# A routed expert layer on one Trainium2 core: weight splits of short and double units, a third branch place, and a copy outside its branch

## The chip, the cores and the metric

One of the eight cores of a Trainium2 chip runs the whole program, once per launch. The metric is the device time of that execution in microseconds (us). Engines: TensorE (PE), VectorE (DVE), ScalarE (ACT), GpSimd (POOL), and SyncE (SP), which issues most transfers.

## The reference

Three layers in a row. An attention between 2048 tokens and 128 states gives 2176 rows of 512; a dense layer follows; then a layer with eight experts, of which each row uses the one with the highest score:

```python
def _moe2_ref(x, expert_emb, tau, w1, w2):
    ...
    expert_idx = np.argmax(logits, axis=1)
    ...
    for e in range(E):
        mask = expert_idx == e
        ...
        h = np.maximum(x[mask] @ w1[e], 0.0)
        out[mask] = gate_w[mask, None] * (h @ w2[e])
```

Here x is 2176 x 512, w1[e] 512 x 1024 and w2[e] 1024 x 512, all float32. For the inputs timed here the experts get 568, 519, 0, 544, 512, 32, 0 and 1 rows.

## The kernel before

A float32 product is made from rounded parts: every operand is split into a high part (ACT copies it to `fp32r`, line 80) and a low part (DVE subtracts, line 81), and three matmuls high x high, low x high, high x low are added up in PSUM (`mm3`, lines 112 to 114).

The routed layer works in **units** U of up to 256 rows of one expert. Unit 0 and 1 are planned early. From unit 2 on the units' experts and shapes are numbers that the chip works out itself, and every engine branches on them (`tc.If`). A unit is **double** (129 or more rows, kind 2), single (65 to 128, kind 1) or **half** (up to 64, kind 0). With the row counts above the units are, in order, with the expert in brackets: 2 double (0), 3 half (3), 4 half (0), 5 double (4), 6 double (1), 7 double (4), 8 half (1), 9 half (5), 10 double (3), 11 half (7), 12 double (3). Unit 12 (`END`) is the last.

Each unit does, in the order of the program: PE turns the next unit's gathered rows (`xt_turns`, `gt<-ident,xg`); the first product h = x W1 (`chosen(U, 0)`); then `middle`: the next unit's x is split into `xth`, `xtl` by ACT and DVE (`xt_split`), GpSimd gathers rows for a later unit, and `fill(U, 0)` splits weights for later units; then the second product y (`chosen(U, 1)`), scaling by the gate (`scale`, tile `ys`) and scattering; then `fill(U, 1)`, the last piece of the weight split. In a double unit (`double_up`) the first product is made in four groups of 24 matmuls in three PSUM banks, each followed by `grouped`: ReLU on ACT (`hth`, line 1147) and the low part on DVE (`htl`, line 75). In a single or half unit (`single_up`) x is the stationary operand, h comes in two halves of 512 columns, ACT copies each out (`hs`, line 1221), PE turns it (`turn`, line 1229 for halves), and ACT and DVE make `hth` from that. A half unit keeps high and low parts of its 64 rows side by side in the 128 lanes, so that the two halves of y must be added at the end: ACT copies the upper 64 lanes (line 1254), DVE adds them (line 1255).

The weights are held in two places, of which unit U uses number U % 2. A unit with a new expert needs W1 (`w1h`, `w1l`, four pieces of 128 x 1024) and W2 (`w2h`, `w2l`, four pieces) split before; the unit ahead does that, steered by a code `due_[U]`: 3 splits W1 and W2 for unit U+1, 2 splits W2 alone (W1 was made one unit earlier), 1 splits W1 for unit U+2, 0 nothing. `fill(U, 0)` makes W1 and three pieces of W2, `fill(U, 1)` the fourth. The codes, and the experts that SP is to fetch next (`fetch`), are computed by DVE in `codes` and lie in the table `plan_`. Instructions of an engine run in the program's order; nothing reorders them here.

Of the kernel before, what the change touches and what calls it, by code (L numbers as in the profile page):

```python
# [11 lines left out]
I32 = mybir.dt.int32  # L12
# [44 lines left out]
def body(tc, x, state, w_in, w_out, ee, tau, w1, w2, out):  # L57
# [58 lines left out]
    with stack:  # L116
# [583 lines left out]
        ctl = rt.tile([P, 2, NU], I32, name="ctl")  # L700
        plan_ = dots.rearrange("p t e -> p (t e)")[:, P // 2 : P // 2 + 3 * NU].bitcast(I32).rearrange("p (r u) -> p r u", r=3)
        ef = rt.tile([P, NU], F32, name="ef")
# [113 lines left out]
        def plan():  # L816
# [87 lines left out]
            def codes():  # L904
# [117 lines left out]

        def fetch(U):

            for part in (1, 2):
                cell = plan_[0:1, part, U : U + 1]
                code = nc.values_load(cell, engines=[ET.SP], min_val=0, max_val=NE)
                with tc.If(code < NE):
                    fetch_part(nc.values_load(cell, engines=[ET.SP], min_val=0, max_val=NE - 1), part)

        PIECES = range(3), range(3, 4)

        def fill(U, half):

            with tc.If(due_[U] > 1):
                if not half:
                    with tc.If(due_[U] > 2):
                        split_all(U + 1, 1)
                split_all(U + 1, 2, PIECES[half])
            if U + 2 <= END:  # L1040
                with tc.If(due_[U] == 1):  # L1041
                    split_all(U + 2, 1, PIECES[half])
# [11 lines left out]

        kind, kp, kf, due_, hT, HP = {}, {}, {}, {}, [], P // 2
        fold = dots.rearrange("p t e -> p (t e)")[:, 0:HP]

        def kinds(U):

            kind[U] = nc.values_load(ctl[0:1, 1, U : U + 1], engines=UENG, min_val=0, max_val=2, skip_runtime_bounds_check_because=BOUND)  # L1060
            kp[U], kf[U] = (bass.RuntimeValue.of_register_unchecked(bass.RegisterHandles([kind[U].val[e] for e in engines]), min_val=0, max_val=2) for engines in ([ET.PE], FENG))

        def dues(U):
            if U < END:
                due_[U] = nc.values_load(plan_[0:1, 0, U : U + 1], engines=FENG, min_val=0, max_val=3, skip_runtime_bounds_check_because=BOUND)

# [63 lines left out]
        def ends(U):  # L1130
            if U == END:
                ix_[U] = [dots[:, NT - 1, r : r + 1].bitcast(I32) for r in range(2)]
# [69 lines left out]
        def double_out(U):  # L1202
            for r in range(1 if U == END else 2):
                down(U, [r])
                scale(U, r)
                scatter(U, r)

        def second(U):
            q = U % 2
            return [(hth[U][k // 4][:, k % 4 * P : (k % 4 + 1) * P], htl[U][k // 4][:, k % 4 * P : (k % 4 + 1) * P], W2H[q, k // 2][:, k % 2, :], W2L[q, k // 2][:, k % 2, :]) for k in range(NFE)]  # L1210

        def single_up(U):
            q, y, ts = U % 2, y_[U][0], second(U)
            h, tr = hs_[U], (hq[U][2], hq[U][0])

# [3 lines left out]

            def leave(m):  # L1220
                A.activation(h[m], hq[U][m], AF.Copy)

            def turn(m):
                with tc.If(kp[U] > 0) as w:
                    for k in range(4):
                        T.transpose(tr[m][:, k * P : (k + 1) * P], h[m][:, k * P : (k + 1) * P], ident)
                with w.Else():
                    for k in range(4):
                        T.matmul(tr[m][:, k * P : k * P + HP], h[m][:, k * P : (k + 1) * P], fold, start=True, stop=True)
                with tc.If(kf[U] > 0) as w:  # L1230
                    positive(hth[U][m], htl[U][m], tr[m])
                with w.Else():
                    positive(lanes(hth[U][m], 0), lanes(hth[U][m], 1), lanes(tr[m], 0))

            high(hq[U][0], terms(0), True)
            low(U, hq[U][0], terms(0))
            leave(0)
            high(hq[U][1], terms(1), True, range(5))
            turn(0)
            high(hq[U][1], terms(1), False, range(5, 8))  # L1240
            low(U, hq[U][1], terms(1))
            leave(1)
            high(y, ts[0:4], True, range(4))
            turn(1)
            high(y, ts[0:4], False, range(4, 8))
# [202 lines left out]
        with tc.manual_schedule():  # L1448
# [68 lines left out]
            kinds(2)  # L1517
            middle(1)
            store(1)
            fill(1, 1)  # L1520
            fetch(1)
            nblk = nc.values_load(ctl[0:1, 1, 0:1], min_val=UMIN, max_val=NU)
            for U in range(2, U1):
# [5 lines left out]
                with cond(U):  # L1529
# [22 lines left out]
            for g in LATE:  # L1552
                late.enter_context(tc.If(nblk > g[0]))
                for U in g:
# [12 lines left out]
                    ends(U)  # L1567
                    chosen(U, 1)
            late.close()
            for r in range(2):  # L1570
# [29 lines left out]
```

## Time and profile before

| | us |
|---|---|
| median of 3 runs | 698.29 (697.58 to 699.22) |
| profiled execution | 694.48 |
| its span, first to last instruction | 692.6 |
| PE busy in the span | 664.3 (96%) |
| DVE, ACT, POOL busy | 480.8, 437.8, 196.6 |

The rows further down come from the profiled execution. In a timeline a row gives the start, the duration, engine, line, operation, what it writes and reads, its count, and in brackets how long the engine was idle before it and what ended that. Matmuls overlap: the time that PE takes for one is the step from its start to that of the next.

### The profile page before, as it was taken

What the parts mean: (1) busy time and instruction counts of PE and PEld (TensorE: products, weight loads), DVE (VectorE), ACT (ScalarE), POOL (GpSimd) and SP (SyncE); (2) the same over time, 40 slices, a digit from 0 to 9 for tenths busy, and PEclk for the clock granted to TensorE, in tenths of its full rate; (3) what the DMA queues carried; (4) which work ended last, traced back from release to release, by engine and by line L of the source; (5) the groups of instructions that cost most, each with busy time, mean ns of one, the idle gap of its engine ahead of it and who ended that gap; (6) DMA issues with size and microseconds to landing.
All of it is one profiled execution on the core that took longest, in us unless ns stands there. A gap on an engine that the chain in (4) does not pass through costs nothing. (4 is left out here: it accounts for less than half of the span.)

```text
span 692.6 us, 11937 instructions
## 1 busy us (share of the span) xinstructions
PE 664.3 (96%) x3833; PEld 565.5 (82%) x3833; DVE 480.8 (69%) x1044; ACT 437.8 (63%) x771; POOL 196.6 (28%) x165
## 2 busy tenths in 40 slices
PE   8898999999999999999999999999989999988995
PEld 8798887777888888888887878998868889767794
DVE  5987798989567786586669888995655722357731
ACT  5877998999788767766786777520544512245520
POOL 2777265553000130030014041233243220332101
PEclk9989999999999999999999999999999999999998
DMA  7663053432010254441122356445695370554401
GB/s 191 158 160 118 32 149 121 126 122 62 1 61 1 59 140 108 92 85 38 62 77 61 131 167 187 126 108 183 207 361 188 120 254 31 186 155 145 166 3 35
DMA packets 58239, 82.71 MB, mean 119 GB/s; under 512 B 25050, under 2 KB 35802, under 8 KB 58148
## 3 DMA queue, kind: packets, MB, share of 16 engines
q1 hardware_dynamic: 54388, 70.31, 34.3%
q0 software_dynamic: 3760, 11.30, 5.0%
q8 instruction: 43, 0.70, 0.4%
q14 instruction: 48, 0.39, 0.2%
HBM read 65.32 MB, written 13.65 MB: 114 GB/s over the span
## 5 line engine op out<-in xcount | busy, mean ns | idle before, releaser
L112 PE MATMUL acc<-woh,gh 128*128 128x512 f32 x272 | 108.5, 403 | 2.0 <-ACT gh L80 1.6
L113 PE MATMUL acc<-wol,gh 128*128 128x512 f32 x272 | 107.5, 396 | 0.0
L114 PE MATMUL acc<-woh,gl 128*128 128x512 f32 x272 | 93.9, 398 | 0.9 <-DVE gl L81 0.9
L112 PE MATMUL hp<-xth,w1h 128*128 128x256 f32 x256 | 72.6, 284 | 1.2 <-DVE htl L75 1.2
L114 PE MATMUL hp<-xth,w1l 128*128 128x256 f32 x256 | 72.1, 281 | 1.5 <-DVE w1l L81 1.5
L113 PE MATMUL hp<-xtl,w1h 128*128 128x256 f32 x256 | 71.9, 281 | 0.6 <-DVE xtl L81 0.6
L1147 ACT ACTIVATE hth<-hp 128x512 fp32r<-128x512 f32 (+1 forms) x34 | 17.8, 533 | 72.7 <-PE hp L114 53.1
L112 PEld LDWEIGHTS acc<-woh,gh 128*128 128x128 f32 x272 | 51.2, 188 | 14.9 <-ACT gh L80 5.0
L523 ACT ACTIVATE er<-h,mb__104 128x512 f32<-128x512 f32 x68 | 46.5, 684 | 25.5 <-PE h L114 22.0
L114 PEld LDWEIGHTS acc<-woh,gl 128*128 128x128 f32 x272 | 50.6, 188 | 14.6 <-DVE gl L81 3.9
L113 PEld LDWEIGHTS acc<-wol,gh 128*128 128x128 f32 x272 | 51.2, 188 | 10.1
L529 DVE TENSOR_TENSOR er<-er 128x512 f32<-128x512 f32 x56 | 40.3, 720 | 21.6 <-ACT er L523 20.9
L1053 POOL DMA_INDIRECT xg<-x1d,perm x26 | 36.4, 1399 | 65.6 <-DVEq L1041 12.8
L552 ACT ACTIVATE h<-er,mb__104 128x512 f32<-128x512 f32 x68 | 47.3, 695 | 8.4 <-DVE er L529 4.8
L112 PE MATMUL h<-xh,mh 128*128 128x512 f32 x128 | 51.3, 401 | 0.4 <-ACT xh L80 0.4
L113 PE MATMUL h<-xl,mh 128*128 128x512 f32 x128 | 50.7, 396 | 0.4 <-DVE xl L81 0.4
L114 PE MATMUL h<-xh,ml 128*128 128x512 f32 x128 | 50.5, 394 | 0.0
L553 ACT ACTIVATE er<-er,mb__104 128x512 f32<-128x512 f32 x68 | 49.3, 725 | 1.4
L114 PEld LDWEIGHTS hp<-xth,w1l 128*128 128x128 f32 x256 | 48.2, 188 | 2.1 <-DVE w1l L81 2.1
L1162 POOL DMA_INDIRECT out<-ys,ix x19 | 22.3, 1176 | 96.8 <-DVE ix L1165 25.7
L112 PEld LDWEIGHTS hp<-xth,w1h 128*128 128x128 f32 x256 | 48.2, 188 | 1.6 <-DVE htl L75 1.4
L113 PEld LDWEIGHTS hp<-xtl,w1h 128*128 128x128 f32 x256 | 48.2, 188 | 0.9 <-DVE xtl L81 0.8
(486 smaller groups left out, 1740.9 us busy)
## 6 DMA issues: line engine op xcount, KB each, us to landing
w<-in_moe_w_in SPq DMA_DIRECT2D x16, 512.0 KB, 4.1
w<-in_moe_w_out SPq DMA_DIRECT2D x16, 512.0 KB, 3.5
es<-in_moe_w SPq DMA_DIRECT2D x32, 256.0 KB, 2.9
sg<-in_moe_w SPq DMA_DIRECT2D x12, 512.0 KB
sd<-in_moe_w SPq DMA_DIRECT2D x12, 512.0 KB
se<-in_moe_w SPq DMA_DIRECT2D x12, 512.0 KB
xn<-in_x SPq DMA_DIRECT2D x32, 128.0 KB, 3.3
md<-mr SPq DMA_DIRECT2D x28, 128.0 KB, 2.4
```

What stands on the lines that cost most here:

```text
L112: T.matmul(o, lh, rh, start=first, stop=False)
L113: T.matmul(o, lh, rl, start=False, stop=False)
L114: T.matmul(o, ll, rh, start=False, stop=last)
L523: A.activation(z, h, AF.Tanh, scale=0.5, bias=mb_[:, 0:1])
L529: V.tensor_tensor(out=z, in0=z, in1=z, op=ALU.mult)
L552: A.activation(r, z, AF.Square, scale=QS, bias=mb_[:, 1:2])
L553: behind["ACT"] = A.activation(z, z, AF.Square, scale=QS, bias=mb_[:, 2:3])
L1053: G.indirect_dma_start(out=xg[U][r], out_offset=None, in_=x1d[: (T1 if U < U0 else NT) * P + 1, :], in_offset=bass.IndirectOffsetOnAxis(ap ...
L1147: A.activation(hi, i, AF.Relu)
L1162: G.indirect_dma_start(out=out[:, :], out_offset=bass.IndirectOffsetOnAxis(ap=ix_[U][r], axis=0), in_=ys_[U][r], in_offset=None, bounds_ch ...
```

## The change

Four things change.

First, `codes` knows two more codes. Where unit U is half or single (`kk` below 2), unit U+1 is double, and the old code is 2 or more, the new code is 7 minus the old one: 4 for 3, 5 for 2. With 4, `fill` splits W1 alone; with 5, nothing. W2 is split inside the double unit instead, after its second group. A fourth row of `plan_` holds the experts whose W2 is then fetched later, inside that double unit.

Second, the unit's branch on its shape stands in three places: `chosen(U, 1)` is the second product alone, `chosen(U, 2)` scaling and scattering. In a half unit the turning of the second half of h moves from the first place to the second, so that on ACT and DVE it stands behind `xt_split` and ahead of `fill(U, 0)`, which moved out of `middle`; the register loads of `kinds` and `dues` come ahead of `fill(U, 0)` too.

Third, ACT's copy of the upper half of y stands ahead of `scale`, outside the branch on half units, which only DVE takes now.

Fourth, the row numbers of unit `END` get tiles of their own, since the fourth row of `plan_` takes their place.

```diff
@@ codes
-                tt(plan_[:, 0, 0 : NU - 2], a[:, 1 : NU - 1], soon[:, 2:NU], ALU.add)
+                tt(b[:, 0 : NU - 2], a[:, 1 : NU - 1], soon[:, 2:NU], ALU.add)
+                V.tensor_copy(plan_[:, 0, 0:U0], b[:, 0:U0])
+                c, put, other = b[:, U0 : NU - 2], room(NL - 2), room(NL - 2)
+                tsc(put, kk[:, 0 : NL - 2], 2.0, ALU.is_lt)
+                stt(put, kk[:, 1 : NL - 1], 2.0, put, ALU.is_ge, ALU.mult)
+                stt(put, c, 2.0, put, ALU.is_ge, ALU.mult)
+                stt(other, put, 7.0, c, ALU.mult, ALU.subtract)
+                tt(plan_[:, 0, U0 : NU - 2], other, c, ALU.max)
...
-                tsc(plan_[:, 2, 1 : NU - 2], a[:, 2 : NU - 1], float(NE), ALU.add)
+                tt(other, a[:, U0 + 1 : NU - 1], put, ALU.mult)
+                tsc(plan_[:, 3, U0 : NU - 2], other, float(NE), ALU.add)
+                tsc(plan_[:, 2, 1:U0], a[:, 2 : U0 + 1], float(NE), ALU.add)
+                stt(plan_[:, 2, U0 : NU - 2], a[:, U0 + 1 : NU - 1], float(NE), other, ALU.add, ALU.subtract)
@@ fill
-                    with tc.If(due_[U] > 2):
+                    with tc.If(due_[U] > 2), tc.If(due_[U] < 5):
                         split_all(U + 1, 1)
-                split_all(U + 1, 2, PIECES[half])
+                with tc.If(due_[U] < 4):
+                    split_all(U + 1, 2, PIECES[half])
@@ chosen, double_up, double_out
-                (double_up, double_out)[j](U)
+                (double_up, double_out, double_end)[j](U)
             with w.Else():
-                (single_up, single_out)[j](U)
+                (single_up, single_out, single_end)[j](U)
...
                 grouped(U, j)
+                if j == 1 and U0 < U <= END:
+                    with tc.If(due_[U - 1] > 3):
+                        split_all(U, 2)
 
         def double_out(U):
+            down(U, range(1 if U == END else 2))
+
+        def double_end(U):
             for r in range(1 if U == END else 2):
-                down(U, [r])
                 scale(U, r)
                 scatter(U, r)
@@ single_out, single_end
         def single_out(U):
             o, ts = y_[U][0], second(U)
+            high(o, ts[0:4], True, range(4))
+            turn(U, 1)
+            high(o, ts[0:4], False, range(4, 8))
             high(o, ts[4:8], False)
             low(U, o, ts)
+
+        def single_end(U):
+            o, t, y, g = y_[U][0], hs_[U][0], ys_[U][0], gt_[U][0]
+            A.activation(t[0:HP], o[HP:P], AF.Copy)
             scale(U, 0)
-            with tc.If(kf[U] < 1):
-                t, y, g = hs_[U][0], ys_[U][0], gt_[U][0]
-                A.activation(t[0:HP], o[HP:P], AF.Copy)
+            with tc.If(kd[U] < 1):
                 stt(y[0:HP], t[0:HP], g[0:HP, 0:1], y[0:HP], ALU.mult, ALU.add)
             scatter(U, 0)
@@ middle
-                fill(U, 0)
@@ the loop over units
                     chosen(U, 0)
+                    if U0 < U < END:
+                        fetch(U - 1, [3])
                     middle(U)
+                    chosen(U, 1)
                     if U < END:
+                        fill(U, 0)
                         ends(U)
-                    chosen(U, 1)
+                    chosen(U, 2)
                     if U < END:
                         fill(U, 1)
```

The turning itself became a function of its own (`turn(U, m)`); its body is the old one.

Where it stands, on ACT at the end of a unit (the code of unit 3; every unit has the same). Before, from the end of `fill(U, 0)` to the fourth piece of W2, `hs<-y` being the copy of the upper half of y:

```order
L1060 TENSOR_LOAD ctl
L1065 TENSOR_LOAD dots
L1192 COMPARE_AND_BRANCH
L1192 UNCONDITIONAL_BRANCH [waits Activation_49]
L1184 UNCONDITIONAL_BRANCH
L1252 COMPARE_AND_BRANCH
L1254 ACTIVATE hs_6012<-y_6004 64x512 [waits DVE_49,PE_49,Activation_49]
L1252 UNCONDITIONAL_BRANCH
L1252 UNCONDITIONAL_BRANCH [waits Activation_49]
L1192 UNCONDITIONAL_BRANCH
L1035 COMPARE_AND_BRANCH
L80 ACTIVATE w2h_4709<-se_5336 128x1024 [waits DMAHW4_49]
```

And with the change:

```order
L1203 COMPARE_AND_BRANCH
L1203 UNCONDITIONAL_BRANCH [waits Activation_49]
L1267 ACTIVATE hs_6028<-y_6020 64x512 [waits PE_49,Activation_49]
L1269 UNCONDITIONAL_BRANCH
L1203 UNCONDITIONAL_BRANCH
L1045 COMPARE_AND_BRANCH
L1049 COMPARE_AND_BRANCH
L80 ACTIVATE w2h_4709<-se_5345 128x1024 [waits DMAHW4_49]
```

The copy no longer waits for DVE, its branch and the two register loads are gone from here, and the piece of W2 has one branch more around it.

On PE, from the last matmul of the same unit to the turning of the next x. Before:

```order
L1188 MATMUL y_5609<-wz 128x1
L1184 UNCONDITIONAL_BRANCH
L1252 UNCONDITIONAL_BRANCH
L1192 UNCONDITIONAL_BRANCH
L1035 UNCONDITIONAL_BRANCH
L1041 UNCONDITIONAL_BRANCH
L1028 UNCONDITIONAL_BRANCH
L1083 MATMUL gt_5995<-ident,xg_5482 128x128 [waits DMASW2_49,DVE_49,PE_49]
```

And with the change:

```order
L1199 MATMUL y_5621<-wz 128x1
L1195 UNCONDITIONAL_BRANCH
L1045 UNCONDITIONAL_BRANCH
L1052 UNCONDITIONAL_BRANCH
L1203 COMPARE_AND_BRANCH
L1203 UNCONDITIONAL_BRANCH
L1269 UNCONDITIONAL_BRANCH
L1203 UNCONDITIONAL_BRANCH
L1045 UNCONDITIONAL_BRANCH
L1052 UNCONDITIONAL_BRANCH
L1038 UNCONDITIONAL_BRANCH
L1094 MATMUL gt_6011<-ident,xg_5491 128x128 [waits DMASW2_49,DVE_49,PE_49]
```

A comparison and three jumps more stand between the two matmuls (not all of the rows are passed in one run: the two sides of a branch follow each other). On DVE, inside a double unit (unit 3's copy of that code), the split of W2 now stands between the low parts of the second and the third group:

```order
L75 SCALAR_TENSOR_TENSOR htl_6025<-hp_6018,hth_6024 128x512 [waits Activation_49]
L1213 COMPARE_AND_BRANCH
L81 TENSOR_TENSOR w2l_5024<-sd_5341,w2h_5023 128x1024 [waits DMAHW1_49,Activation_49]
L81 TENSOR_TENSOR w2l_5034<-sd_5344,w2h_5033 128x1024 [waits DMAHW2_49,Activation_49]
L81 TENSOR_TENSOR w2l_5202<-se_5342,w2h_5201 128x1024 [waits DMAHW3_49,Activation_49]
L81 TENSOR_TENSOR w2l_5239<-se_5345,w2h_5238 128x1024 [waits DMAHW4_49,Activation_49]
L1213 UNCONDITIONAL_BRANCH
L1213 UNCONDITIONAL_BRANCH [waits DVE_49]
L75 SCALAR_TENSOR_TENSOR htl_6027<-hp_6019,hth_6026 128x512 [waits Activation_49]
```

Before, the two rows of line 75 follow each other.

## Rows read from the trace of the kernel before

**Rows 1.** The page, busy time, share of the span and instructions per engine.

```profile
PE 664.3 (96%) x3833; PEld 565.5 (82%) x3833; DVE 480.8 (69%) x1044; ACT 437.8 (63%) x771; POOL 196.6 (28%) x165
```

**Rows 2.** By stretch: length, busy PE, PEld, DVE, ACT, POOL, PE clock, DMA.

```profile
512.50:527.07 14.57, 12.54 (x62) 9.76 (x61) 7.90 (x14) 6.99 (x11) 4.14 (x3) 0.88 0.71 258
574.60:598.07 23.47, 23.37 (x150) 20.81 (x149) 8.43 (x15) 6.75 (x10) 5.68 (x4) 1.00 0.31 108
608.83:624.38 15.55, 12.51 (x62) 9.48 (x61) 8.21 (x14) 6.97 (x11) 5.09 (x3) 0.89 0.56 172
624.38:651.63 27.25, 24.44 (x152) 21.06 (x151) 22.21 (x29) 16.80 (x22) 3.99 (x3) 1.00 0.52 178
651.63:662.71 11.08, 10.80 (x60) 8.41 (x59) 4.30 (x9) 2.94 (x6) 2.02 (x2) 1.00 0.14 50
...
616.00:619.00 3.00, 2.96 (x13) 2.34 (x13) 0.67 (x2) 0.38 (x1) 1.14 (x1) 0.58 0.91 245
```

**Rows 3.** Timeline of PE in units 4, 9 and 10, around its waits.

```profile
518.51 1.10 PE L1229 MATMUL hp<-dots,hs 128*128 128x64 f32 x8 [1.79 <-ACT hs L1221]
...
612.66 0.39 PE L1180 MATMUL hp<-w1l,xth 128*128 128x512 f32 x1
616.04 1.57 PE L1229 MATMUL hp<-dots,hs 128*128 128x64 f32 x8 [2.99 <-ACT hs L1221]
...
626.16 0.39 PE L114 MATMUL hp<-xth,w1l 128*128 128x256 f32 x1 [0.44 <-DVE w1l L81]
...
627.29 0.38 PE L114 MATMUL hp<-xth,w1l 128*128 128x256 f32 x1 [0.51 <-DVE w1l L81]
...
628.43 0.39 PE L114 MATMUL hp<-xth,w1l 128*128 128x256 f32 x1 [0.52 <-DVE w1l L81]
...
637.18 0.39 PE L112 MATMUL hp<-xth,w1h 128*128 128x256 f32 x1 [1.24 <-DVE htl L75]
```

**Rows 4.** Timeline of ACT, end of unit 8 and in unit 9.

```profile
608.67 1.04 ACT L80 ACTIVATE w2h<-se 128x1024 fp32r<-128x1024 f32 x1
613.45 0.59 ACT L1254 ACTIVATE hs<-y 64x512 f32<-64x512 f32 x1 [3.74 <-DVE ys L67]
...
615.39 0.60 ACT L1221 ACTIVATE hs<-hp 128x512 f32<-128x512 f32 x1 [0.41 <-ACTq L1041]
...
621.69 1.08 ACT L80 ACTIVATE xth<-gt 128x512 fp32r<-128x512 f32 x2
622.64 2.02 ACT L80 ACTIVATE w1h<-sg 128x1024 fp32r<-128x1024 f32 x2
```

**Rows 5.** Timeline of DVE, the same places.

```profile
610.12 1.22 DVE L81 TENSOR_TENSOR w2l<-se,w2h 128x1024 fp32r<-128x1024 f32 x1
612.52 0.15 DVE L1165 CAST ix<-gg 128x1 int32<-128x1 f32 x1 [1.18 <-issue]
612.59 0.74 DVE L67 TENSOR_SCALAR ys<-y,gg 128x512 f32<-128x512 f32 x1
...
622.31 1.29 DVE L81 TENSOR_TENSOR xtl<-gt,xth 128x512 fp32r<-128x512 f32 x2
623.52 0.23 DVE L1110 COPY gg<-xg 128x2 f32<-128x2 f32 x2
623.75 2.36 DVE L81 TENSOR_TENSOR w1l<-sg,w1h 128x1024 fp32r<-128x1024 f32 x2
```

**Rows 6.** Timelines of DVE and PE ahead of unit 2: `codes`, x split, first use.

```profile
470.93 0.18 DVE L72 TENSOR_TENSOR dots<-ph 128x16 int32<-128x16 f32 x1
...
475.44 1.29 DVE L81 TENSOR_TENSOR xtl<-gt,xth 128x512 fp32r<-128x512 f32 x2 [0.85 <-ACTq L1041]
...
479.04 0.29 PE L113 MATMUL hp<-xtl,w1h 128*128 128x256 f32 x1
```

**Rows 7.** Timeline of PE, end of unit 5.

```profile
550.68 0.40 PE L114 MATMUL y<-w2h,ht 128*128 128x512 f32 x1
550.91 1.04 PE L1083 MATMUL gt<-ident,xg 128*128 128x128 f32 x8
```

**Rows 8.** Timeline of PE, second product of unit 7, sixth and seventh matmul.

```profile
587.70 0.40 PE L114 MATMUL y<-w2h,htl 128*128 128x512 f32 x1
588.20 0.47 PE L112 MATMUL y<-w2h,hth 128*128 128x512 f32 x1
```

More of the change, by code (lines that the diff above doesn't have):

```diff
@@ L1021, in early_split, with fetch @@
                 early_fetch()
-        def fetch(U):
-            for part in (1, 2):
+        def fetch(U, rows=(1, 2)):
+            for part in rows:
                 cell = plan_[0:1, part, U : U + 1]
@@ L1028, in fetch @@
                 with tc.If(code < NE):
-                    fetch_part(nc.values_load(cell, engines=[ET.SP], min_val=0, max_val=NE - 1), part)
+                    fetch_part(nc.values_load(cell, engines=[ET.SP], min_val=0, max_val=NE - 1), min(part, 2))
         PIECES = range(3), range(3, 4)
@@ L1053, in gather @@
                 G.indirect_dma_start(out=xg[U][r], out_offset=None, in_=x1d[: (T1 if U < U0 else NT) * P + 1, :], in_offset=bass.IndirectOffsetOnAxis(ap=perm[:, c : c + 1], axis=0))
[L1055 removed]
+        kind, kp, kf, kd, due_, hT, HP = {}, {}, {}, {}, {}, [], P // 2
         fold = dots.rearrange("p t e -> p (t e)")[:, 0:HP]
@@ L1060, in kinds @@
             kind[U] = nc.values_load(ctl[0:1, 1, U : U + 1], engines=UENG, min_val=0, max_val=2, skip_runtime_bounds_check_because=BOUND)
-            kp[U], kf[U] = (bass.RuntimeValue.of_register_unchecked(bass.RegisterHandles([kind[U].val[e] for e in engines]), min_val=0, max_val=2) for engines in ([ET.PE], FENG))
+            kp[U], kf[U], kd[U] = (bass.RuntimeValue.of_register_unchecked(bass.RegisterHandles([kind[U].val[e] for e in engines]), min_val=0, max_val=2) for engines in ([ET.PE], FENG, [ET.DVE]))
         def dues(U):
             if U < END:
-                due_[U] = nc.values_load(plan_[0:1, 0, U : U + 1], engines=FENG, min_val=0, max_val=3, skip_runtime_bounds_check_because=BOUND)
+                due_[U] = nc.values_load(plan_[0:1, 0, U : U + 1], engines=FENG, min_val=0, max_val=5, skip_runtime_bounds_check_because=BOUND)
         def xt_tiles(U, parts=range(2)):
@@ L1131, in ends @@
             if U == END:
-                ix_[U] = [dots[:, NT - 1, r : r + 1].bitcast(I32) for r in range(2)]
+                ix_[U] = [rt.tile([P, 1], I32, name=f"ixe{r}") for r in range(2)]
                 ys_[U] = [ep.tile([P, DM + 2], F32, tag="xg", bufs=2, name=f"yse{r}")[:, 0:DM] for r in range(2)]
@@ L1210, in second, with turn @@
             return [(hth[U][k // 4][:, k % 4 * P : (k % 4 + 1) * P], htl[U][k // 4][:, k % 4 * P : (k % 4 + 1) * P], W2H[q, k // 2][:, k % 2, :], W2L[q, k // 2][:, k % 2, :]) for k in range(NFE)]
+        def turn(U, m):
+            tr, h = hq[U][(2, 0)[m]], hs_[U][m]
+            with tc.If(kp[U] > 0) as w:
+                for k in range(4):
+                    T.transpose(tr[:, k * P : (k + 1) * P], h[:, k * P : (k + 1) * P], ident)
+            with w.Else():
+                for k in range(4):
+                    T.matmul(tr[:, k * P : k * P + HP], h[:, k * P : (k + 1) * P], fold, start=True, stop=True)
+            with tc.If(kf[U] > 0) as w:
+                positive(hth[U][m], htl[U][m], tr)
+            with w.Else():
+                positive(lanes(hth[U][m], 0), lanes(hth[U][m], 1), lanes(tr, 0))
         def single_up(U):
-            q, y, ts = U % 2, y_[U][0], second(U)
-            h, tr = hs_[U], (hq[U][2], hq[U][0])
+            q, h = U % 2, hs_[U]
             def terms(m):
@@ L1218, in terms @@
                 return [(*(wide2(t[U][k // 2])[:, k % 2, 0:P] for t in (xth, xtl)), W1H[q, k][:, fs], W1L[q, k][:, fs]) for k in range(KT)]
[L1220 to L1233, printed above, removed]
             high(hq[U][0], terms(0), True)
             low(U, hq[U][0], terms(0))
-            leave(0)
+            A.activation(h[0], hq[U][0], AF.Copy)
             high(hq[U][1], terms(1), True, range(5))
-            turn(0)
+            turn(U, 0)
             high(hq[U][1], terms(1), False, range(5, 8))
             low(U, hq[U][1], terms(1))
[L1242 to L1245, printed above, removed]
+            A.activation(h[1], hq[U][1], AF.Copy)
         def single_out(U):
             o, ts = y_[U][0], second(U)
+            high(o, ts[0:4], True, range(4))
+            turn(U, 1)
+            high(o, ts[0:4], False, range(4, 8))
             high(o, ts[4:8], False)
             low(U, o, ts)
+        def single_end(U):
+            o, t, y, g = y_[U][0], hs_[U][0], ys_[U][0], gt_[U][0]
+            A.activation(t[0:HP], o[HP:P], AF.Copy)
             scale(U, 0)
-            with tc.If(kf[U] < 1):
-                t, y, g = hs_[U][0], ys_[U][0], gt_[U][0]
-                A.activation(t[0:HP], o[HP:P], AF.Copy)
+            with tc.If(kd[U] < 1):
                 stt(y[0:HP], t[0:HP], g[0:HP, 0:1], y[0:HP], ALU.mult, ALU.add)
```

4 lines of the change are left out of this document (3 added, 1 removed).

## The prediction

> **What bounds the kernel now.** First the page's list of busy time: TensorE (PE) is busy for 96% of the span [rows 1]. Where PE hardly pauses, what ScalarE (ACT) and VectorE (DVE) do counts only where PE waits for them. So the second view is one row of time per unit of the routed part [rows 2], to be read as pairs of equal work. Units 4, 9 and 11 are halves ahead of a double one and issue the same matmuls: unit 11 takes 11.08 us, unit 4 14.57 and unit 9 15.55. They lose 3.49 and 4.47. Units 7 and 10 are doubles ahead of a half one: 23.47 and 27.25, so unit 10 loses 3.78. The three losses come to 11.74 us, all of them where halves stand next to splits of weights. The clock column says that units 4 and 9 also ran part of their time slowly (0.88 and 0.89 of the full clock).
>
> Third, PE's own waits inside these units [rows 3]. In units 4 and 9 one wait stands out, 1.79 and 2.99 us, both for ACT's copy `hs` of the first 512 columns of h. [...] In unit 10 there are three waits of about half a microsecond for the low parts of W1, 1.47 together, and one of 1.24 us, in front of its last group, for `htl`.
>
> Fourth, why ACT is late for unit 9 [rows 4, 5]. ACT ends its third piece of W2 at 609.71, and y of unit 8 is complete before that, since unit 9's matmuls begin at 608.83 [rows 2]. Its next work, copying the upper half of y, starts only at 613.45, held for 3.74 us by DVE's scaling of y. DVE is splitting W2 until 611.34 and spends 1.18 us more on branches and register loads. Behind the copy stands the fourth piece of W2 (1.04 us) and only then `hs` (615.39, 0.60 us). Unit 4 begins in the same order, with W1 pieces in place of W2's.
>
> **The change, part by part.**
>
> *The copy outside its branch.* The order rows show it: the copy of y waits for PE and ACT and no more for DVE. For unit 9: the copy starts about 610.0 (609.71 and a gap like the 0.41 in front of `hs` now [rows 4]) and ends at 610.6; fourth piece until 611.7; 0.41; `hs` from 612.1 to 612.7. PE's fifth matmul of the second bank starts at 612.66 [rows 3] and takes a quarter of a microsecond, so `hs` is in time, and the 2.99 us go, with the slow stretch behind them. What is late next is DVE: its third W2 piece ends at 611.34, the gap of 1.18 shrinks to something between 0.4 (two register loads now come earlier) and 1.2, then 0.8 for index and scaling, 0.9 for the added half (as long as the scaling) with its branch, 1.3 for the fourth piece [rows 5]. That is 614.8 to 615.6. The low part of unit 9's first h tile can follow only then, and takes 0.35 more; PE would be ready for it at about 614.75. So a new wait of 0.3 to 1.2 us; I take 0.4, since the loads were most of that gap. It costs no clock: the wait of 1.24 us in unit 10 left that unit's clock at 1.00 [rows 2, 3]. Unit 4 goes the same way; its pieces are W1's and end earlier against PE, residue 0.3.
>
> *The split in three places.* In a half unit the ReLU of the second h tile now stands behind the split of the next unit's x. Its cover: from the second `hs` copy on, PE has 2.2 us of matmuls and turning before that ReLU could start; ACT needs 0.6 and 1.08 in that time [rows 4], DVE 1.29 and 0.23 behind ACT [rows 5]. ACT fits, DVE is late by up to 0.3 us. I charge 0.2 to each of units 4 and 9, and 0.1 to each of units 3, 8 and 11. If the cover failed, the whole x split, 1.5 us, would be paid. In return the next weights' split starts right behind the ReLU. In unit 9 ACT's first W1 piece begins at 622.64, behind the x split, and DVE's at 623.75; now ACT starts where the x split stood, 621.7, and 0.35 later for its branches, and DVE's first piece 1.05 after that, at 623.1: 0.6 earlier against the end of the unit. Of the 1.47 us of W1 waits in unit 10 those 0.6 go and 0.9 stays: DVE's pace of 1.14 us a piece is what it was.
>
> *W2's split left to the double unit.* By the rule in the code this happens where a half is followed by a double with a new expert: unit 4 before 5 (code 5), unit 9 before 10 (code 4). In unit 10 the wait of 1.24 us [rows 3] comes from DVE, which has four pieces of W2 between W1 and the first group's `htl`. With them behind group 1, group 0's part is done well before the last group wants the bank: the wait goes. The new work behind group 1, ACT 4 x 1.0 and DVE 4 x 1.14, ends some 6.6 us after that group, while two groups (2 x 2.9 us) run; W2's first piece is wanted after these, the last one 1.4 us later still. Covered, by 0.6 us at the last piece; without that cover PE would wait the difference. Unit 5 brings nothing by itself. The fetch of the next W2 moves behind this split: SP issues it in unit 5 or 10 when DVE has freed the buffers, and it is wanted some 5 us into the second product; W1 comes first. Free, unless four transfers of 512 KB take over 8 us.
>
> *More codes.* Nine more small DVE operations of 0.18 to 0.2 each delay the x split for unit 2 by 1.8 us, from 476.7 to 478.5; PE wants it at 479.0 [rows 6]. Hidden with half a microsecond to spare. Should each cost twice as much, 1.3 us show.
>
> *PE's third branch.* No row shows it alone. From below: at a unit's end PE passes several jumps now, and the turning starts 0.23 after the last matmul, the step of any other matmul [rows 7]: 0. From above, the one step of PE that nothing explains, 0.50 instead of 0.23 at the seventh matmul of a double's second product [rows 8]: 0.27 x 11 units = 3.0. I take 0, by the row that is nearest in kind. [...] The unit ends of the trace, which show no time for the jumps they have, speak for hidden.
>
> **The sum.** Unit 4: 3.49 - 0.3 - 0.2 = 3.0. Unit 9: 4.47 - 0.4 - 0.2 = 3.9. Unit 10: 1.24 + 0.6 = 1.85, and with it a third of the 1.07 us that no wait there holds (3.78 - 1.47 - 1.24): 2.2. Less 0.3 for units 3, 8 and 11: 8.8 us. The profiled execution took 694.48 and would come to 685.7; the median of the runs is 698.29, 3.8 above it, and I set the sum against the median: **689.5 us**.
>
> **Rivals.**
> 1. *The wait changes its owner.* DVE is behind ACT everywhere, and if its gap behind the W2 pieces stays at 1.2 us and the second ReLU is late by as much, units 4 and 9 keep 1.5 to 2 us each, with some slow clock: gain 4.5 to 6, time 692.3 to 693.8. For it: DVE's chain above has no slack. Against it: it starts earlier.
> 2. *The third place costs PE 0.27 us a unit*: gain 5.8, time 692.5. For it only [rows 8].
> 3. *The codes never come to 4 or 5* (the change doesn't do what it says): unit 10 keeps its wait for `htl`; gain 7.4, time 690.9. Against it: both pairs of units are there in [rows 2].
> 4. *Slower:* each unit's end now takes PE over one more body that it does not run, in 11 units. If PE's instructions then come late, it pays at each; from 0.8 us (8.8 / 11) on the gain is gone, and at 1.2 us a unit, the length of DVE's gap among its branches [rows 5], the time is 702.7. Against it: unit ends show no pause [rows 7]. [...]
>
> **How the numbers follow.** Forecast 0.70, rival 1 0.12, rival 2 0.07, rival 3 0.06, rival 4 0.05. What a measurement can tell from no change is about 0.2%, 1.4 us. The range's lower end has all losses gone: 698.3 - 11.9 = 686.4, 11.9 being the 11.74 and the little that unit 5 may give; the upper end takes in rivals 1 to 3 at 694.0. Rival 4 lies from 696 to 703: a part of it, with stray cases of the others, counts as no change. Faster 0.92, same 0.03, slower 0.05.
>
> **What would show it.** Right: in units 4 and 9 no wait of PE for `hs` over half a microsecond and a clock of 1.00; the copy of y on ACT ahead of DVE's scaling; W2's four pieces between the second and third group of units 5 and 10; unit 10 at about 25 us, its W1 waits shorter but there. Wrong: units 3, 8 and 11 longer by over 0.3 us, a step over 0.4 where a unit ends, a new wait of PE for `hth` of a microsecond or more, or waits for W2 at the start of the second product of units 5 and 10.

## The result and the profile after

The changed kernel takes **703.67 us** (median of 22 runs, 699.47 to 709.33) where the kernel before takes 699.34 on the same chips (22 runs, 697.09 to 705.39): a ratio of 1.0056 with a 95% interval of 1.0033 to 1.008. It is slower by some 4 us, 0.6%; the forecast was 689.5, and the range (686.4 to 694.0) does not hold the result.

The profiled execution took 701.9 us, with a span of 700.0. The busy line of the page, as [rows 1]:

```profile
PE 663.7 (95%) x3833; PEld 566.0 (81%) x3833; DVE 483.4 (69%) x1053; ACT 439.1 (63%) x771; POOL 187.6 (27%) x165
```

PE does the same work, 663.7 against 664.3 us, in a longer span. Busy time by unit of the changed kernel, the columns of [rows 2]; the rows are units 2, 4, 5, 7, 9, 10 and 11:

```profile
480.40:505.39 24.99, 23.49 (x150) 21.09 (x149) 13.21 (x20) 10.89 (x14) 5.92 (x6) 1.00 0.70 236
516.21:529.38 13.17, 11.23 (x62) 8.38 (x61) 7.43 (x14) 5.29 (x9) 3.84 (x4) 1.00 0.69 242
529.38:555.12 25.74, 23.84 (x154) 21.46 (x154) 18.25 (x22) 15.45 (x19) 4.88 (x3) 1.00 0.49 166
580.43:605.40 24.97, 23.47 (x150) 21.08 (x149) 8.34 (x15) 6.75 (x10) 4.00 (x4) 1.00 0.32 108
616.22:628.13 11.91, 10.83 (x61) 8.45 (x61) 8.87 (x15) 7.68 (x12) 1.94 (x1) 1.00 0.67 208
628.13:657.31 29.18, 25.53 (x151) 22.37 (x151) 20.90 (x26) 16.47 (x21) 2.97 (x3) 0.94 0.46 167
657.31:668.46 11.15, 10.81 (x60) 8.42 (x59) 5.03 (x11) 2.94 (x6) 2.02 (x2) 1.00 0.14 51
```

The halves did as forecast or nearly: unit 9 falls from 15.55 to 11.91, unit 4 from 14.57 to 13.17, unit 11 grows by 0.07. Units 4 and 9 run at the full clock now (1.00); unit 10 no longer does (0.94, see *Late W2* below). The loss sits where nothing was expected, in the doubles: unit 7, which splits no W2 at all, takes 24.97 instead of 23.47. PE's waits in the routed part (operation, whom it waits for, us in total, times, longest) name the place:

```profile
PE y L112 <- DVE ht L75: 9.2, 5, 2.8
PE y L1191 <- DVE hth L75: 1.7, 5, 0.4
PE y L112 <- DVEq L1203: 1.5, 1, 1.5
PE hp L1191 <- issue: 1.1, 1, 1.1
PE y L1191 <- ACT hs L1255: 1.1, 1, 1.1
```

The first and the third row are one wait in each of the six doubles, 1.5 us in four of them, 1.9 in unit 5 and 2.8 in unit 10. Unit 7 shows it, on PE's timeline (last matmul of the first product, first of the second), then on DVE's:

```profile
592.37 0.28 PE L114 MATMUL hp<-xth,w1l 128*128 128x256 f32 x1
594.15 0.47 PE L112 MATMUL y<-w2h,hth 128*128 128x512 f32 x1 [1.50 <-DVE ht L75]
...
593.32 0.69 DVE L75 SCALAR_TENSOR_TENSOR ht<-hp,ht 128x512 fp32r<-128x512 f32 x1 [2.19 <-ACT ht L1158]
```

The first matmul of `y` reads `hth` of the *first* group, which ACT had ended at 584.70, some 9 us earlier. It starts only when DVE has ended the subtraction of the *last* group, `ht` (594.01). Before, the same matmul followed the first product without a pause, and it was the seventh matmul of the second product that came late, by the step of 0.50 of [rows 8]. Unit 6 of the kernel before, on PE (last matmul of the first product, first and seventh of the second) and on DVE:

```profile
562.94 0.28 PE L114 MATMUL hp<-xth,w1l 128*128 128x256 f32 x1
563.06 0.39 PE L112 MATMUL y<-w2h,hth 128*128 128x512 f32 x1
...
564.72 0.47 PE L112 MATMUL y<-w2h,hth 128*128 128x512 f32 x1
...
563.88 0.69 DVE L75 SCALAR_TENSOR_TENSOR ht<-hp,ht 128x512 fp32r<-128x512 f32 x1 [2.12 <-ACT ht L1147]
```

`ht` ends at 564.57 and the seventh matmul starts 0.15 later; in the changed kernel the first starts 0.14 behind `ht`. The wait for `ht` now stands six matmuls earlier.

Unit by unit, routed part (PE's first turning of unit 2 to its last matmul): before 207.40, after 212.75. Units 4 and 9 gain 1.40 and 3.6; units 3, 8 and 11 cost 0.06 each; the six doubles cost 1.63, 1.9, 1.6, 1.5, 1.9 and 1.6, together 10.2. The remaining 2.0 us of the difference of the spans lie ahead of the routed part; 1.8 of them are there two turnings earlier (443.92 against 442.10), ahead of the new codes, where the code is nearly the same (see *before_again* below).

### The profile page after: what moved, and what is told of

It reads as the page before. It is cut to its first block, busy times and chain, and to the rows that moved or that the text cites. A ratio compares the mean times of both kernels' runs of the same rounds, so it can differ in the third digit from the quotient of the medians.

```text
span 700.0 us, 12162 instructions
## 1 busy us (share of the span) xinstructions
PE 663.7 (95%) x3833; PEld 566.0 (81%) x3833; DVE 483.4 (69%) x1053; ACT 439.1 (63%) x771; POOL 187.6 (27%) x165
## 5 line engine op out<-in xcount | busy, mean ns | idle before, releaser
L1173 POOL DMA_INDIRECT out<-ys,ix x19 | 20.1, 1057 | 117.4 <-DVE ix L1176 53.1
L112 PE MATMUL y<-w2h,hth 128*128 128x512 f32 x96 | 39.4, 411 | 10.7 <-DVE ht L75 9.2
```

The lines of the kernel that those rows point to most:

```text
L112: T.matmul(o, lh, rh, start=first, stop=False)
L1173: G.indirect_dma_start(out=out[:, :], out_offset=bass.IndirectOffsetOnAxis(ap=ix_[U][r], axis=0), in_=ys_[U][r], in_offset=None, bounds_ch ...
```

## The experiments

Two theories stood at first. **Counts** (a reading of the built program; no trace shows a count, and the runs below test it): PE's matmuls wait for a count of VectorE's instructions (`DVE_49` in the order rows), which this program brings to the same value on the two sides of a branch, so a wait behind the branch asks for a value that both sides reach. In the short side (a single or half unit) the change leaves a single subtraction in the first place, which carries the whole count. In the built program (unit 3's copy) that instruction adds 8 at once, as many as the eight instructions of the double's side bring one by one (four subtractions, four pieces of late W2), and PE's first `y` matmul in the double waits for the full count. Before, the short side had two subtractions, adding 3 and 1; PE's first `y` matmul then asked for the third of four, long there, and its seventh for the fourth: the step of [rows 8]. **Jumps:** three branch places cost PE's instruction stream time by themselves.

Time is the median in us; the routed part and the units come from PE's timeline of one profiled execution each (7 is a double without any split of W2 of its own).

| kernel | time | routed | unit 4 | 5 | 7 | 9 | 10 |
|---|---|---|---|---|---|---|---|
| before | 699.3 | 207.40 | 14.57 | 23.84 | 23.47 | 15.55 | 27.25 |
| changed | 703.7 | 212.75 | 13.17 | 25.74 | 24.97 | 11.91 | 29.18 |
| e1_turn_back | 698.2 | 204.65 | 12.39 | 25.15 | 23.59 | 12.50 | 27.40 |
| e2_pad1 | 697.8 | 207.01 | 12.78 | 27.76 | 23.04 | 12.10 | 29.38 |
| e3_pad3 | 692.2 | 203.92 | 11.75 | 29.59 | 23.04 | 11.72 | 25.87 |
| e5_copy_only | 693.4 | 201.20 | 12.22 | 23.85 | 23.48 | 12.63 | 26.26 |
| e6_copy_pad | 692.7 | 200.03 | 12.26 | 23.50 | 23.26 | 12.95 | 25.95 |
| e7_three_no_late | 686.7 | 196.73 | 11.67 | 23.40 | 23.04 | 11.93 | 25.00 |
| e8_code4_only | 698.2 | 209.80 | 12.24 | 32.86 | 23.04 | 11.72 | 28.06 |
| e10_rows_no_codes | 697.4 | 207.13 | 12.22 | 33.20 | 23.04 | 11.72 | 25.03 |
| e11_no_pad_no_late | 700.2 | 209.78 | 12.90 | 25.36 | 24.99 | 11.98 | 26.78 |
| e12_row3_before_w1 | 707.9 | 216.94 | 20.11 | 23.40 | 23.04 | 11.72 | 28.05 |
| e13_one_memset | 687.1 | 197.91 | 12.53 | 23.40 | 23.04 | 12.01 | 25.00 |
| before_again | 699.2 | 209.11 | 14.70 | 23.85 | 23.48 | 16.99 | 27.28 |

**e1_turn_back: one part undone.** The second turn goes back into the first place; the three places stay.

```diff
-        def single_out(U):
             o, ts = y_[U][0], second(U)
             high(o, ts[0:4], True, range(4))
             turn(U, 1)
             high(o, ts[0:4], False, range(4, 8))
+
+        def single_out(U):
+            o, ts = y_[U][0], second(U)
```

> The changed kernel with one part undone: the turning and ReLU of the second h tile of a short unit stand in the first branch place again; three places, the new codes and the copy outside its branch stay. Theory C (counts): after a branch PE waits for a count of DVE's instructions that must hold for both sides; in the changed kernel the short side's only DVE instruction of the first place carries the place's last count, and in a double unit that count is reached with the last group, so PE waits 1.5 us or more ahead of the second product in units 2, 5, 6, 7, 10 and 12. Here the short side has two DVE instructions again, so the count is that of the third group: the six waits go, the step of 0.50 at the seventh matmul comes back in each double, 6 x 1.4 = 8 us less than the changed kernel, about 695 to 696, ratio to before 0.993 to 0.997. Rival J (jumps): the six waits are the fetch of PE's instructions for a further branch place; three places are still there, so they stay and the time stays at 702 to 704.

Measured: 698.19 us, ratio 0.9981 (0.9953 to 1.0009). Unit 7 returns to 23.59, with the third place still there: the jumps are not the cost. The time missed the expected 695 to 696 by 2 us: units 5 and 10 still take 25.15 and 27.40, and PE waits there for the third group's `htl` (1.3 and 1.6 us), behind which the late W2 stands.

**e2_pad1 and e3_pad3: the count alone.** One or three tiny DVE memsets at the end of the short side of the first place; nothing else differs from the changed kernel.

```diff
+            for r in range(1):
+                V.memset(pad_[:, r : r + 1], 0.0)
```

(e2; 3 in e3.)

> The changed kernel with one DVE memset of one column added at the end of a short unit's side of the first place, and nothing moved. C: the first matmul of the second product waits for the third group's low part: waits gone in units 2, 6, 7 and 12 (1.5 us each), part of it left in units 5 and 10, where W2's split stands ahead of the third group; no step of 0.50 at the seventh matmul either. 6 to 9 us less than the changed kernel: 694 to 697. J: one memset in a side that no double unit runs changes nothing, 702 to 704.

> As before, with three memsets, so that the count is that of the first group. C: the waits go in all six doubles, the first product's end and the second's start follow each other in units 2, 6, 7 and 12, and in units 5 and 10 at most some 0.7 us for ACT or for W2 are left: about 10 us less than the changed kernel, 692.5 to 695, ratio to before 0.990 to 0.994. J: 702 to 704.

Measured: 697.80 (ratio 0.9967, 0.994 to 0.9994) and 692.17 (0.9878, 0.9815 to 0.9942). The memsets stand on the short side, which a double unit does not run, and yet unit 7 falls to 23.04 with either, 0.44 below the kernel before: the step of [rows 8] is gone as well. That is the theory of the counts, and instructions on a side that a double unit doesn't run can hardly reach it in another way. A second sign: with one memset PE's count is that of the third group, so it should still wait for `htl` where W2's split stands ahead of that group, and it does, 2.6 us in unit 5 and 3.1 in unit 10 of e2; with three memsets no wait for `htl` is left. But unit 5 now takes 27.76 and 29.59.

**e5_copy_only and e6_copy_pad: the other part alone.** The kernel before with the copy ahead of the scaling and outside its branch, and this with one memset more.

```diff
+            t, y, g = hs_[U][0], ys_[U][0], gt_[U][0]
+            A.activation(t[0:HP], o[HP:P], AF.Copy)
             scale(U, 0)
-            with tc.If(kf[U] < 1):
-                t, y, g = hs_[U][0], ys_[U][0], gt_[U][0]
-                A.activation(t[0:HP], o[HP:P], AF.Copy)
+            with tc.If(kd[U] < 1):
```

> The kernel before, with one part of the change alone: ACT's copy of the upper half of y ahead of the scaling and outside the branch. The sum's first step alone: the wait for hs of 2.99 us in unit 9 goes and about 0.3 to 1.2 us of a wait for hth comes, unit 9 at 12 us in place of 15.55; unit 4 between 12 and 13 in place of 14.57; unit 10 as it was or a little better: 4.5 to 6 us less than before, 693.5 to 695. If the copy was not what held PE up (DVE would have been late all the same): units 4 and 9 within 1 us of before, 698 to 699.

> The kernel before with the copy outside its branch (as in e5_copy_only) and one small DVE memset more at the end of the short side of the first branch place. The theory of the counts: the memset takes the last of the four counts of VectorE, so that in a double unit the 7th matmul of the second product no longer waits for the last group's subtraction; the step of 0.3 to 0.5 us goes in all six double units. Expected: double units 23.05 (23.45, 23.85, 23.68, 23.48 in e5_copy_only), unit 10 about 25.9, halves as in e5_copy_only, routed part 201.2 - 2.3 = about 199, time 691.1 (693.4 less 2.3). If the step is not a wait for a count (a cost of the weight load or of the tile), doubles stay at 23.4 to 23.9 and the time at 693.4.

Measured: 693.39 (ratio 0.9887, 0.9823 to 0.995) and 692.65 (0.99, 0.9872 to 0.9927). The copy brings 6.2 us of the routed part: 2.35 in unit 4, 2.9 in unit 9, 1.0 in unit 10. In unit 9 ACT's copy no longer stands behind DVE's scaling; here, in e5, it is ahead of it (ACT, then DVE):

```profile
613.94 0.59 ACT L1252 ACTIVATE hs<-y 64x512 f32<-64x512 f32 x1 [1.02 <-PE hp L1180]
...
615.74 0.15 DVE L1165 CAST ix<-gg 128x1 int32<-128x1 f32 x1 [1.18 <-issue]
615.81 0.74 DVE L67 TENSOR_SCALAR ys<-y,gg 128x512 f32<-128x512 f32 x1
```

The memset of e6 takes 0.2 to 0.35 off units 2, 5, 6, 7 and 10, not the 0.4 expected; by the medians the two kernels can't be told apart.

**e7, e8 and e10: what the late W2 costs.** Unit 5 of e3_pad3 takes 6 us longer than before, and two theories stood: the late pieces themselves, or the added row of fetches, which SyncE (SP) passes without a transfer in most units. e7 is e3 without codes and row, e10 keeps the row and never sets a code, e8 sets code 4 alone.

```diff
-                stt(put, c, 2.0, put, ALU.is_ge, ALU.mult)
+                stt(put, c, 9.0, put, ALU.is_ge, ALU.mult)
```

(e10; 3.0 in e8.)

> The changed kernel with three memsets in the short side of the first place (as in e3_pad3) and without any late W2: no codes 4 and 5, no third row of fetches. Three branch places and the copy outside its branch stay. Theory: three places cost nothing once the counts are even; the late W2 is what makes unit 5 cost 29.6 instead of 23.5 in e3_pad3. Expected: unit 5 23.1 to 23.5, unit 4 12.2, unit 9 12.4, unit 10 25.0 to 25.9, routed part 198 to 199, time 689.5 to 691. The rival, that the third place or the moved fill costs unit 5 its time: unit 5 stays above 27 and the time at 692 or above.

> e3_pad3 with the codes 4 and 5 never set: the added row of fetches is passed without a transfer in every unit, the late split is never taken. Against e7_three_no_late it prices the skipped row of fetches and the tests of the late codes by themselves. Late split (L): as e7_three_no_late within 1 us, unit 5 23.1 to 23.5. Skipped fetches (S): W1 of unit 6, issued at 513 to 519 us in the kernel before, is issued after 520 us again, and unit 5 or 6 costs 1 to 5 us over e7_three_no_late.

> e3_pad3 with the late W2 only behind a short unit of due code 3 (here unit 9 into unit 10); unit 4 keeps its old code 2, the added fetches are passed without a transfer everywhere but for unit 10. Two theories of unit 5. Late split (L): the late pieces on ACT and DVE between two of unit 5's groups are the cost; then unit 5 falls to 23.1 to 23.5, unit 4 is 12.2, units 9 and 10 stay at 11.7 and 25.9, routed part 198.2, time about 687. Skipped fetches (S): SP passes the added fetch late, and what is fetched behind it comes late in either case; then some unit from 5 to 7 still costs 1 us or more over e7_three_no_late.

Measured: e7 686.74 (ratio 0.9828, 0.9794 to 0.9862), e10 697.36 (0.9974, 0.9948 to 0.9999), e8 698.22 (0.9989, 0.9963 to 1.0015). e7 is faster than expected (689.5 to 691). Between e7 and e10 lie the row of fetches, not taken in any unit, and the tests of the codes: 10.6 us, 9.8 of it in unit 5, where 1 to 5 were expected. The late split was expected to be the cost (L); unit 5 has it without any late piece. The chain in e10, on SP (W2 for unit 5, then W1 for unit 6), ACT (W2 for unit 5) and PE, and the DMA's share between (next to last column):

```profile
510.56 1.82 SPq L987 DMA_DIRECT2D sd<-in_moe_w  x2
513.26 1.64 SPq L987 DMA_DIRECT2D se<-in_moe_w  x2
524.58 1.04 SPq L984 DMA_DIRECT2D sg<-in_moe_w  x2
...
536.35 2.00 ACT L80 ACTIVATE w2h<-sd 128x1024 fp32r<-128x1024 f32 x2 [11.29 <-SPq L1039]
...
537.22 0.28 PE L114 MATMUL hp<-xth,w1l 128*128 128x256 f32 x1
545.05 0.58 PE L112 MATMUL hp<-xth,w1h 128*128 128x256 f32 x1 [7.55 <-DVE htl L75]
```

```profile
520.00:524.00 4.00, 3.67 (x24) 3.01 (x22) 2.08 (x6) 1.96 (x4) 1.72 (x1) 1.00 0.40 144
524.00:530.00 6.00, 5.62 (x37) 4.56 (x36) 1.31 (x5) 0.39 (x1) 1.92 (x2) 1.00 0.69 234
530.00:534.00 4.00, 4.00 (x36) 4.00 (x35) 0.00 (x0) 0.00 (x0) 0.00 (x0) 1.00 0.80 307
534.00:536.00 2.00, 2.00 (x19) 2.00 (x18) 0.00 (x0) 0.00 (x0) 0.00 (x0) 1.00 0.02 8
```

SP issues W2 for unit 5 from 510.56 to 514.90, its data have been there since about 522, and W1 of unit 6 goes out at 524.58; in the kernel before it went out at 512.94. ACT's wait for W2 of unit 5 does not end with these data: the trace names SP's line 1039, the branch of the fetch, and ACT stands still for 11.29 us until W1 has come too and the DMA is quiet (share 0.02 from 534 to 536), and everything behind it on ACT and DVE with it, PE in unit 5 at last for 7.55. That a skipped fetch waits for the transfers ahead of it, and a later reader for the skip, is the author's reading of the built program; the trace shows these times alone, and e12 tests it. Behind PE's wait the granted clock is 0.50 from 545 to 549, and a matmul takes 0.21 where 0.12 is usual, which is most of what unit 5 loses beyond the wait. In the changed kernel unit 5 waits only 1.90 us, 0.4 more than the other doubles: it begins at 529.38, 5.2 us later than in e3_pad3 (524.15), so PE comes to the same release later (ACT begins unit 5's late pieces at 536.20 in e3, after 4.64 us of waiting for SP, and at 536.80 in the changed kernel, without a wait). That is why the gains of e2 and e3 ahead of unit 5 came back as a longer unit 5.

e8 against e10 prices the late pieces of unit 10 at 3.0 us: 28.06 against 25.03. The pieces are held by SP and by each other, and the last two groups' `hth` stand behind them on ACT:

```profile
641.34 1.06 ACT L80 ACTIVATE w2h<-se 128x1024 fp32r<-128x1024 f32 x1 [0.82 <-SPq L1039]
643.73 1.06 ACT L80 ACTIVATE w2h<-se 128x1024 fp32r<-128x1024 f32 x1 [1.33 <-DVE w2l L81]
644.69 0.58 ACT L1159 ACTIVATE hth<-hp 128x512 fp32r<-128x512 f32 x1
...
645.33 0.50 PE L112 MATMUL y<-w2h,hth 128*128 128x512 f32 x1 [1.74 <-ACT hth L1159]
```

The wait of 1.74 us is little more than half of the price. Behind it the granted clock is 0.50 from 647 to 649, and nine matmuls from 645.33 to 649.02 take 1.6 us more than nine steps of 0.23. e3_pad3 has the same pieces; PE waits 1.10 us there, the clock of unit 10 stays at 1.00, and the unit takes 25.87. So the late pieces cost unit 10 from 0.8 to 3.0 us.

**e11_no_pad_no_late and e13_one_memset.** e7 without its memsets, and with one.

```diff
-            for r in range(3):
-                V.memset(pad_[:, r : r + 1], 0.0)
```

> e7_three_no_late without its three memsets: the changed kernel's three branch places and its copy, no late W2 and no third row of fetches. In the built program TensorE's first matmul of a double unit's second product waits again for the count that the last group's subtraction brings. Theory of the counts: each of the six double units gets its 1.5 to 1.7 us back, routed part 196.7 + 10 = 206 to 207, time about 696.5, whatever the fetches do. If the count costs this much only together with the late W2, doubles stay below 24 and the time below 690.

> e7_three_no_late with one memset in place of three in the short side of the first place. Theory of the counts: one is enough, since it alone has to come with the last group's subtraction and TensorE's first matmul of the second product then asks for the third group's, which is done 2 us earlier: doubles 23.04, 23.40, 23.36, 23.04, 22.74 (units 2, 5, 6, 7, 12), unit 10 25.0, routed part 196.5 to 197.3, time 686.5 to 688.5. If the three memsets helped by the time that they take on VectorE and not by their count, a third of the step or more comes back: doubles over 23.6.

Measured: 700.21 (ratio 1.0002, 0.9971 to 1.0033) and 687.09 (0.983, 0.9792 to 0.9868). e11 was expected at 696.5 and is slower by nearly 4 us; e13's time came as expected. One memset is worth 13 us by the medians (three together take 0.08 us on DVE). PE's waits in e11 against e7, the same list as above:

```profile
PE y L112 <- DVE ht L75: 7.5, 5, 1.5
PE y L112 <- DVEq L1192: 1.5, 1, 1.5
```

```profile
PE y L1181 <- DVE pad__193 L1244: 2.1, 5, 1.1
PE hp L114 <- DVE w1l L81: 0.8, 2, 0.5
```

Six waits of 1.5 us each, in e7 none. A double costs 1.95 more in all (unit 10 1.77); the pause itself and the slow step behind it hold 1.74 of that (1.78 and 0.31 between matmul starts where 0.12 and 0.23 are usual). In the routed part e11 takes 11.87 us more than e13, nearly 2 for each double.

**e12_row3_before_w1: the order on SP.** e3_pad3 with the added row passed ahead of W1's fetch.

```diff
-                        fetch(U - 1, [3])
+                        fetch(U - 1, [3, 1])
...
-                    fetch(U)
+                    fetch(U, (1, 2) if U < U0 else (2,))
```

> e3_pad3 (late W2 with both codes) with one edit in SyncE's order: the test of the added row of fetches is passed ahead of the fetch of W1 and not behind it. Theory of the skipped fetch (S): ScalarE's wait for W2 of unit 5 no longer takes in the landing of unit 6's W1; unit 5 falls from 29.6 to 23.4 to 24.5, units 4, 9 and 10 stay at 11.7, 11.7 and 25.9 or better, routed part 197 to 199, time 687 to 689. Rival: the order is of no matter, the added test as such delays SP; then unit 5 stays above 28 and the time at 692. A third possibility: W1 comes late in its turn, and units 5 to 7 stand at over 25 each.

Measured: 707.87 (ratio 1.012, 1.0087 to 1.0152). Unit 5 falls to 23.40 as the theory of the skipped fetch says; but the time was missed by 20 us, since W1 now stands behind the skip, and units 4 and 11 pay 20.11 and 19.85. W1 for unit 5 leaves at 515.09 (505.17 in e10), and ACT waits for SP with it, ahead of the `hs` that PE wants:

```profile
519.78 1.06 ACT L80 ACTIVATE w1h<-sg 128x1024 fp32r<-128x1024 f32 x1 [6.42 <-SPq L1039]
...
526.90 1.97 PE L1236 MATMUL hp<-dots,hs 128*128 128x64 f32 x8 [6.77 <-ACT hs L1251]
```

In both orders what stands behind the skip on SP came late, W1 of unit 6 in e10 (524.58) and W1 of unit 5 here; the order only chose what.

**before_again: the spread.**

> The kernel before, unchanged, for a second profile of it and as a measure of the spread: the ratio should hold 1 in its interval. The first profiled execution took 694.5 us where the median of the timed ones is 698.6 to 699.5. If the 4 to 5 us between them lie ahead of the routed part, this profile has a routed part within 0.5 of 207.4 again and starts it up to 5 us later; if they lie in the routed part, it shows 209 to 212 there.

Measured: 699.21 (ratio 0.9979, 0.9946 to 1.0012); its profiled span is 704.1, 11.5 above the first profile's. Of these 9.7 lie ahead of the routed part (it starts at 488.08, not 478.37) and 1.7 in it, 1.45 of them in unit 9. In unit 9 PE's wait for `hs` is the same (2.97 against 2.99), and the stretch at a granted clock of 0.50 behind it is longer (627 to 631; in the first profile 617 to 619, then 0.54 from 619 to 620). Neither half of the expectation holds to the letter. Between these two executions most of the spread comes from the part ahead, so units are to be compared, not single spans, and a unit that ran slowly in part, as unit 9 of the kernel before, is known to some 1.5 us only.

**The sum of the parts**, in the routed part: 207.40 before; the copy takes 6.20 (201.20, e5); three places with the moved split add 8.58 (209.78, e11), which is the count's 13.05 (e11 less e7; 1.24 of it is a pause in unit 4, see the last section) without the 4.47 that e7 gains on e5; late W2 and its row add 2.97 (212.75). By medians: 699.3, 693.4, 700.2, 703.7. The copy and the three places with one or three memsets, without late W2, give 687: **e7 and e13 beat both kernels**, the one before by 1.7%.

## Why the prediction was wrong

- **The copy outside its branch: right.** Unit 9 was to lose its wait for `hs` and get one of 0.4 for the low part; the wait for `hs` in the turn is gone, and one of 1.07 stands in its place at the start of the second product, where ACT's second `hs` and DVE's `hth` end within 0.1 us of each other (623.05 and 622.97). 3.64 us measured, 3.9 forecast. Unit 4: 1.40 of 3.0, with a wait of 1.10 that no row explains (last section). On ACT, DVE and PE, against [rows 4, 5] and [rows 3]:

```profile
617.23 0.60 ACT L1267 ACTIVATE hs<-y 64x512 f32<-64x512 f32 x1 [0.33 <-PE gt L1094]
...
619.31 0.60 ACT L1250 ACTIVATE hs<-hp 128x512 f32<-128x512 f32 x1 [0.54 <-PE hp L1199]
...
619.01 0.74 DVE L67 TENSOR_SCALAR ys<-y,gg 128x512 f32<-128x512 f32 x1
...
623.13 1.18 PE L1191 MATMUL y<-w2h,hth 128*128 128x512 f32 x4 [1.07 <-ACT hs L1255]
```

  ACT's copy of y is ahead of DVE's scaling, and `hs` follows 2.1 us behind it. DVE's gap ahead of the scaling shrank from 1.18 to 0.41 us, the low end of the forecast's range. In e7 units 4, 9 and 10 gain 2.9, 3.6 and 2.25: 8.8 against the 9.1 that the sum had for these three. In unit 10 that is luck: 1.24 of its forecast was to come from late W2, which e7 does not have.
- **The split in three places: right** as to what it was priced for. Units 3, 8 and 11 cost 0.06 each, 0.1 charged.
- **More codes: right.** The split of x for unit 2 ended 1.64 us ahead of the unit's first turning before (476.73 and 478.37) and ends 0.25 ahead of it now (480.15 and 480.40): 1.4 us later, forecast 1.8, and PE runs into the unit without a pause.
- **PE's third branch: the step that failed.** "I take 0, by the row that is nearest in kind" was right of the jumps (the turning still starts 0.23 after the last matmul) and wrong of the place. The rows that held the answer were [rows 8], "the one step of PE that nothing explains": a wait for the last group's count, already there once in each double. The prediction used its size, 0.27, as a price for a jump, and didn't ask what released the seventh matmul. DVE's `ht` had ended 0.15 us before it (588.05), and the code has two instructions on one side of the branch against four on the other. The move of the second turn takes one of the two away, and the wait moves from the seventh matmul to the first: 1.5 to 1.9 us more in each of six doubles, 10.2 where 0 stood (in units 5 and 10 late W2 has a part in it). The turning at a unit's end, which the term was about:

```profile
554.89 0.39 PE L114 MATMUL y<-w2h,ht 128*128 128x512 f32 x1
555.12 1.04 PE L1094 MATMUL gt<-ident,xg 128*128 128x128 f32 x8
```

  It starts 0.23 after the last matmul, as in [rows 7].
- **Late W2: wrong, and in two places.** The 1.24 us of unit 10 were put down to the four pieces of W2 ahead of `htl`. In e7 W2 is where it was, and the wait is 0.28: DVE comes to unit 10's first `htl` 10.14 us behind the unit's start and not 12.05, since its chain starts 0.9 us earlier and its waits for ACT's copy of y (0.75) and behind it (0.20) are gone. The late pieces bring unit 10 a wait at the start of the second product instead, 1.10 in e3 and 1.74 in e8, and with the count's wait 2.78 in the changed kernel. "Covered, by 0.6 us" had left out the waits of the pieces for SP. And this wait does cost clock, where the 1.90 of unit 5 left that unit's at 1.00: behind it the granted clock is 0.54 from 644.57 to 648.10 (0.50 from 645 to 647), and a matmul takes 0.43 where 0.23 is usual, 1.6 us in all:

```profile
644.57 0.76 PE L112 MATMUL y<-w2h,hth 128*128 128x512 f32 x1 [2.78 <-DVE ht L75]
645.13 0.63 PE L113 MATMUL y<-w2l,hth 128*128 128x512 f32 x1
645.56 0.63 PE L114 MATMUL y<-w2h,htl 128*128 128x512 f32 x1
```

  Last, "Free, unless four transfers of 512 KB take over 8 us" asked only for the transfer that runs, not for the units in which it is skipped: the skip is what costs, 10.6 us between e7 and e10. In the changed kernel late W2 and its row together show as 2.97 only, since PE comes later to the same release.
- **Rival 4** ended on the right side with the wrong mechanism: it put the pause at unit ends, and it had a chance of 0.05. That PE's instructions come late at these ends is not borne out: the turning starts 0.23 after the last matmul there, and e7 has all three places and is the fastest kernel. Whether the pause of the last section is of that kind stays open.

## What to carry to other kernels

Here the two sides of a runtime branch issue different numbers of instructions, and moving instructions on one side changed whom the other side's consumer waits for: 1.5 to 1.9 us in each of six doubles, and one memset on the short side took the wait away again (13 us by the medians, e11 and e13). In a program built like this one, before moving an instruction, list for each consumer which count it asks for, and even the sides with a tiny instruction if need be. Nor was a transfer under a condition free where it was skipped (10.6 us between e7 and e10): what stood behind it on the issuing engine went out late (524.58 in e10, 512.94 in the kernel before), and a reader of older data stood still for 11.29 us. A step in the baseline that nothing explains is to be explained before it is priced.

## What was not expected of the hardware

In unit 4 of the changed kernel PE pauses for 1.10 us in front of one matmul of the first product, and the trace names no releaser. Of the ten kernels with three places seven have it (e2 1.06, e1 0.97, e11 0.82, e13 0.81, e10 0.49, e8 0.29); e3, e7 and e12 do not. e13 and e7 differ by two memsets.

```profile
521.31 0.40 PE L1191 MATMUL hp<-w1l,xth 128*128 128x512 f32 x1 [1.10 <-issue]
```

The DMA's share doesn't tell them apart: 0.95 from 517 to 521.3 here, 0.96 in the same place of e7 (514.6 to 518.95). One thing in the traces does: a transfer of instructions (16 KB, the queue q8) ends 1.2 to 1.6 us before each of the seven pauses ends, 2.4 to 3.8 us behind the start of the unit, and in e3, e7 and e12 it ends 0.8 to 2.0 us behind it, while the matmul in question is due 3.5 us behind it at the earliest. Late instructions are thus a candidate; that they are the cause is not shown, and the trace doesn't say which engine that queue feeds.
